# Threshold attention before a squared-ReLU feed-forward: where the weight sums are widened and multiplied in, and the order of a period's steps

## The chip, the cores and the metric

The kernel runs on one core of one Trainium2 chip, as one launch. The metric is the device time in microseconds; a kernel's time is the median of its runs.

## The reference, cut to what matters

```python
# attention: 8 batches, 8 heads, 576 positions, 64 values per head
scores = q @ k.T / 8                                   # per batch and head
thresh = max(scores, axis=-1) - tau                    # tau = 0.02
scores = where(scores >= thresh, scores, -1e9)
attn = exp(scores - max(scores))
attn = attn / (sum(attn, axis=-1) + 1e-9)
x = (attn @ v) laid out as (4608 tokens, 512)
# feed-forward
h = maximum(x @ w_in, 0)                               # w_in 512 x 2048
out = h * h @ w_out                                    # w_out 2048 x 512
```

The activations are float32. The two feed-forward matrices arrive as 64-bit floats, and the kernel turns them into float32 itself.

## The kernel before

The program has two stages: attention, whose result goes to DRAM as `xT`, and the feed-forward, which reads it back. Everything on the chip is ordered by hand: each engine carries out its instructions in the order in which the program issues them, and waits only for what it needs.

**The feed-forward** computes both layers as a two-level seven-product scheme (`inner`, line 689, called by `hidden_layer`, line 800, and `output_layer`, line 918), with 49 products where 64 would be plain. Its operands are sums of blocks of the matrices and of the inputs. The sums of `w_in` are made by GpSimd during attention: the generator `sums` (line 249) yields 44 additions of 128x512, and `prepare_x` (line 761) 12 more for the first 512 tokens. `sums_step` (line 570) makes one of them. The first layer's matmuls are line 812, the second's line 947.

**Attention** works on 144 units. A unit is 128 query rows of a pair of heads (32 pairs: 4 units each, and for every two pairs one more with the 64 rows that remain of both). `period(p)` (line 607), for p from -2 to 74, handles units A=2p and B=2p+1, and the weights and products of earlier units: m=p-2 is the pair of units whose product is made in this period. For each unit:

- *Scores* (`scores`, line 434): 64x512 matmuls of queries and keys into PSUM, steps `SA` and `SB`. The sign is turned by a scale, so that the largest score is the smallest value.
- *Minimum* (`top`, line 452): VectorE copies the scores of one head from PSUM to SBUF and takes each row's minimum on the way. There are two heads, so `topA0`, `topA1`, `topB0`, `topB1`.
- *Threshold* (`least`, line 459): GpSimd adds tau to the two minima, `leastA`, `leastB`.
- *Power* (line 462): ScalarE takes the exponential, `powA0` to `powB1`.
- *Mask* (line 467): VectorE zeroes what is beyond the threshold and sums the rest per row, `maskA0` to `maskB1`. It needs the power and the threshold.
- *Sum* (lines 474 and 477): `over` adds 1e-9 on GpSimd, `inv` inverts on VectorE, both one period after the masks, for both units at once.
- *Turning the weights* (`fill`, line 499; `half_turn`, line 375): the weights of the two units are 18 blocks of 128x128, turned on TensorE in three groups: `V` (8 blocks) and `W` (2 blocks) in the period after the masks, `U` (8) in the one after that. `V` and `U` share one PSUM tile; `W` uses the PSUM banks 2 and 3 of `sc`. ScalarE copies each group to the SBUF tile `wT` (`filled`, line 523): `eV`, `eW`, `eU`. `wT` has two buffers.
- *The inverse sums* are turned with `W`: eight 64x64 matmuls (line 515) of the inverse sum, spread by a zero step over 64 columns, with the identity. They land beside the two blocks of `W`, and `eW` copies them to blocks 10 and 11 of `wT` (`SCALE_AT`).
- *Product* (`values`, line 532): step `PV`, weights times values into banks 0 and 5 of `sc`.
- *x* (`given_out`, line 634): VectorE multiplies both heads' products by the turned inverse sums while it moves them from PSUM to SBUF (line 638). Then the loads of later values are issued (`valued`), and the outputs to `xT` (`give_x`, issued by `ask`, line 578).

The six banks of `sc` are shared. Scores of A lie in banks 0 and 5 with the rest of their columns in 1 and 4, those of B in 2 and 3 with rests in 1 and 4; the turned queries and keys of the next pair (`T`, line 397, evicted by `eT`, lines 402 and 410) in 1 and 4; `W` in 2 and 3; the product in 0 and 5. The helper `touch` (line 354) makes an instruction wait for those of other engines in the same bank. After `eT` the loads of the queries or keys of a later pair are issued.

The order of a period's steps is one of two lists of names: `CONVERTING` (line 596) for periods 2 to 34, in which 32 blocks of the feed-forward matrices are fetched (`fetch`) and converted in six steps (`c1` and `c2` on ScalarE, `c3` on GpSimd, `c4` and `c5` on VectorE, `c6` on GpSimd, with a write-back by line 247 for half of them), and `PLAIN` (line 592) for the others. In plain periods from 35 on, `s1` makes one of the 56 additions, and up to period 59 `s2` a second one. All DMAs but a few at the start are issued by SyncE (SP), in the order of the program.

Of the kernel before, what the change touches and what calls it, by code (L numbers as in the profile page):

```python
# [48 lines left out]
def kernel(  # L49
# [25 lines left out]
    nc = tc.nc  # L75
# [423 lines left out]
    def fill(m, f, pt, at=None):  # L499

        first, count = FILLS[f]
        if m not in wT:
            wT[m] = sb.tile([P, (2 * CH + 2) * P], FP32, tag="wT", bufs=W_RING, name="wT")
        for i, (u, c) in enumerate(FIRST[first : first + count]):
            half_turn(pt, i, weights[2 * m + u][:, c, :, :].rearrange("p j d -> p (j d)"), at)
        if f == "W":
            rs = smalls.pop(m)
            for j in range(2):
                for r in range(2):
                    rows = ds(r * HALF, HALF)  # L510
                    for u in range(2):
                        one = rs[rows, 3, 2 * u + j : 2 * u + j + 1]
                        wide = bass.AP(tensor=one.tensor, offset=one.offset, ap=[one.ap[0], [0, D]])
                        to = pt[ds(u * D, D), r, ts(count + j, HALF)]
                        made = nc.tensor.matmul(to, wide, ident[rows, rows], start=True, stop=True)  # L515
                        touch("turns", made, at and at + r * BANK, BANK)

    def filled(m, f, pt, at=None):

# [81 lines left out]
    def spots():  # L601
# [5 lines left out]
    def period(p):  # L607

        A, B_, a, b = 2 * p, 2 * p + 1, 2 * p - 2, 2 * p - 1
        m, turns = p - 2, TURNS.get(p, ())  # L610
        late, pt = {"W": []}, {}

        def fills(f, m):
            if has(2 * m):
                pt[f] = pt_pool.tile([P, 2, BANK], FP32, tag="pt", name="pt")
                fill(m, f, pt[f])

        def evict(f, m):
            if has(2 * m):
                filled(m, f, pt[f], 2 * BANK if f == "W" else None)  # L620

        def W():
            if has(2 * m + 2):
                pt["W"] = middle()
                fill(m + 1, "W", pt["W"], 2 * BANK)

        def turn_some():
            late["turn"] = [turn(g // 2, g % 2, spots()) for g in turns]

        def PV():  # L630
            if has(2 * m):
                values(m)

        def given_out():
            if has(2 * m):
                x = sb.tile([P, 2, P], FP32, tag="x", bufs=2, name="x")
                for j in range(2):
                    made = nc.vector.tensor_tensor(  # L638
                        out=x[:, j, :], in0=sc[:, ds(5 * j * BANK, P)], in1=wT[m][:, ts(SCALE_AT + j, P)], op=ALU.mult
                    )  # L640
                    touch("x", made, 5 * j * BANK, P, m)
                wT.pop(m)
                valued(m)
                give_x(m, x)
# [18 lines left out]
        steps = {  # L663
            "U": lambda: fills("U", m), "V": lambda: fills("V", m + 1), "W": W, "T": turn_some,
            "eU": lambda: evict("U", m), "eV": lambda: evict("V", m + 1), "eW": lambda: evict("W", m + 1),
            "eT": lambda: every("turn"),
            "SA": scored_a, "SB": scored_b,
            "PV": PV, "x": given_out,
            "c1": lambda: convert1(begun(p)), "c2": lambda: convert2(begun(p)),
            "c3": lambda: convert3(begun(p - 1)), "c4": lambda: convert4(begun(p - 1)),  # L670
            "c5": lambda: convert5(begun(p - 1)), "c6": lambda: convert6(begun(p - 1)),
            "s1": lambda: sums_due(p) and sums_step(), "s2": lambda: sums_due(p) and p < 60 and sums_step(), "fetch": lambda: fetch(begun(p + 2)),
        }
        steps["over"] = lambda: do(a, "over")
        steps["inv"] = lambda: do(a, "inverse")
        for letter, n in (("A", A), ("B", B_)):
            for what, name in (("least", "least"),):
                steps[what + letter] = lambda n=n, name=name: do(n, name)
            for what, name in (("top", "top"), ("pow", "power"), ("mask", "mask")):
                for j in range(2):  # L680
                    steps[f"{what}{letter}{j}"] = lambda n=n, name=name, j=j: do(n, name, j)
        for name in CONVERTING if converts(p) else PLAIN:
            steps[name]()
        for n in (A, B_):
            if has(n) and units[n][1] == FULL:
                for i in units[n][0]:
                    turned.pop(i)
# [522 lines left out]
```

## Time and profile before

| what | value |
|---|---|
| median of 3 runs | 1318.03 us (1316.82 to 1320.18) |
| span of the profiled execution | 1314.0 us |
| first matmul of layer 1 (line 812) | 519.45 us |
| busy over the span: PE, weight loads, VectorE, ScalarE, GpSimd | 97%, 87%, 77%, 65%, 64% |
| granted TensorE clock, mean | 0.998 |
| mask (line 467) | 288 times, 229.6 us |
| power (line 462) | 288 times, 208.2 us |
| minimum (line 452) | 288 times, 205.5 us |
| product (line 532) | 5760 matmuls, 176.7 us |
| evictions of weights (line 523), 128x1024 | 144 times, 146.6 us |
| x (line 638) | 144 times of 128x128, 285 ns each |
| inverse sums turned (line 515) | 1152 matmuls, 33.2 us |

PE, VectorE, ScalarE and GpSimd (POOL in the profile) work side by side, so their busy times overlap and don't add up to the span. Consecutive instructions of one engine overlap at their ends as well, so a run of them is better read by the distance of their starts than by their durations. In rows of the timeline the first number is the start in microseconds, the second the time from there to the end of the group, then follow engine, line, operation, tiles and shapes; in brackets stands how long the engine was idle before and what it waited for.

### The profile page before, as it was taken

To read this page: it belongs to the slowest core of one execution; us is meant where nothing else is said; L and a number is where in the kernel's file an instruction comes from. 1 tells how busy PE (TensorE), PEld (TensorE's weight loads), DVE (VectorE), ACT (ScalarE), POOL (GpSimd) and SP (SyncE) were. 2 spreads that over 40 slices of the span, in tenths; PEclk is the share of its full clock that TensorE was granted. 3 is DMA by queue.
4 is the path that set the end of the run, shared out by engine and by line. 5 is a ranking of instruction groups with operands and counts; after the bars stand their busy time and mean duration, and the time that the engine had idled before them with its cause. 6 is when DMAs were issued, how large, how long until landed. Compare 5 with 4: busy or idle time off the path is not lost.

```text
span 1314.0 us, 47792 instructions
## 1 busy us (share of the span) xinstructions
PE 1277.6 (97%) x19483; PEld 1141.4 (87%) x19483; DVE 1016.3 (77%) x2497; ACT 849.6 (65%) x1464; POOL 839.0 (64%) x958
## 2 busy tenths in 40 slices
PE   7999999899999999999999999999999999999998
PEld 5666666677777777999999999999999999999998
DVE  5999999999999996877887788777656654665463
ACT  5999999888989886566756675665524322432240
POOL 1444444455555421778987888758777777777775
PEclk9999999999999999999999999999999999999999
DMA  5555566544433322466656655669645135423411
GB/s 135 143 160 142 155 174 182 149 103 99 101 78 86 77 60 46 148 206 192 195 180 210 197 187 179 193 232 394 249 161 161 48 115 162 161 63 100 161 33 33
DMA packets 247035, 192.12 MB, mean 146 GB/s; under 512 B 97184, under 2 KB 195488, under 8 KB 246816
## 3 DMA queue, kind: packets, MB, share of 16 engines
q1 hardware_dynamic: 245360, 188.63, 47.4%
q8 instruction: 153, 2.51, 0.8%
q10 hardware_dynamic: 1456, 0.44, 0.1%
q14 instruction: 66, 0.54, 0.1%
HBM read 116.65 MB, written 72.35 MB: 144 GB/s over the span
## 4 chain that ended last, share of the span: by engine, by line
PE 85%; ACT 8%; DVE 3%; issue 2%; DMA 1%; SPq 1%; POOL 0%; ACTq 0%; DVEq 0%; POOLq 0%
PE ph L812 30%; PE po L947 28%; PE sc L434 9%; PE sc L532 8%; PE pt L379 5%; ACT arena L523 3%; ACT arena L462 3%; PE sc L397 2%; PE sc L515 2%; DVE arena L452 1%; PE sc L379 1%; DMA wall<-w 1%; ACT arena L402 1%; DVE arena L467 0%; DMA arena<-in_k_dram 0%
## 5 line engine op out<-in xcount | busy, mean ns | idle before, releaser
L125 POOL TENSOR_TENSOR arena<-arena 128x512 f32<-128x512 f32 (+1 forms) x314 | 378.0, 1222 | 134.5 <-DVE arena L125 120.5
L947 PE MATMUL po<-wall,arena 128*128 128x128 f32 x3528 | 395.0, 275 | 1.6 <-ACT arena L724 1.4
L947 PEld LDWEIGHTS po<-wall,arena 128*128 128x128 f32 x3528 | 394.3, 192 | 2.2 <-ACT arena L724 1.8
L812 PE MATMUL ph<-arena,wall 128*128 128x128 f32 x3528 | 394.2, 275 | 0.7 <-DVE arena L638 0.7
L812 PEld LDWEIGHTS ph<-arena,wall 128*128 128x128 f32 x3528 | 394.0, 192 | 0.8 <-issue 0.8
L125 DVE TENSOR_TENSOR arena<-ph,arena 128x512 f32<-128x512 f32 x378 | 256.4, 689 | 86.2 <-PE ph L812 66.0
L122 POOL TENSOR_TENSOR arena<-arena 128x128 f32<-128x128 f32 (+2 forms) x314 | 255.2, 814 | 48.6 <-DMA arena<-w 31.9
L125 DVE TENSOR_TENSOR arena<-po,arena 128x128 f32<-128x128 f32 x378 | 108.4, 290 | 167.6 <-PE po L947 163.4
L467 DVE SCALAR_TENSOR_TENSOR arena<-arena 128x576 f32<-128x576 f32 x288 | 229.6, 817 | 2.7 <-ACT arena L462 1.7
L462 ACT ACTIVATE arena<-arena 128x576 f32<-128x576 f32 x288 | 208.2, 778 | 14.1 <-DVE arena L452 7.0
L452 DVE TENSOR_SCALAR_CACHE_REDUCE arena<-sc 128x576 f32<-128x576 f32 x288 | 205.5, 751 | 13.3 <-ACT arena L523 5.5
L758 ACT COPY c<-arena 128x512 f32<-128x512 f32 (+1 forms) x303 | 173.5, 579 | 50.4 <-DVE arena L122 41.3
L532 PEld LDWEIGHTS sc<-arena 64*64 64x64 f32 x5760 | 154.0, 133 | 55.3 <-DVE arena L452 28.7
L532 PE MATMUL sc<-arena 64*64 64x128 f32 (+1 forms) x5760 | 176.7, 263 | 18.1 <-DVE arena L452 11.6
L122 DVE TENSOR_TENSOR arena<-arena,c 128x512 f32<-128x512 f32 (+1 forms) x267 | 174.9, 663 | 6.1 <-ACT c L758 4.0
L434 PE MATMUL sc<-arena 64*64 64x64 f32 (+1 forms) x2304 | 167.4, 414 | 5.6 <-ACT arena L402 5.6
L523 ACT COPY arena<-pt 128x1024 f32<-128x1024 f32 x144 | 146.6, 1018 | 24.8 <-PE pt L379 24.4
L724 ACT COPY arena<-po 128x128 f32<-128x128 f32 x63 | 16.6, 264 | 186.4 <-PE po L947 183.7
L459 POOL TENSOR_SCALAR arena<-arena,tau_p 128x2 f32<-128x2 f32 x144 | 75.1, 521 | 73.4 <-DVE arena L452 67.8
L724 ACT COPY arena<-ph 128x512 f32<-128x512 f32 x63 | 36.6, 581 | 124.2 <-PE ph L812 123.5
L379 PEld LDWEIGHTS pt<-ident,arena 64*128 64x128 f32 x2304 | 83.1, 139 | 38.2 <-ACT arena L523 25.6
L434 PEld LDWEIGHTS sc<-arena 64*64 64x64 f32 x2304 | 59.2, 134 | 52.2 <-ACT arena L402 26.4
(46 smaller groups left out, 896.1 us busy)
## 6 DMA issues: line engine op xcount, KB each, us to landing
g<-arena SPq DMA_DIRECT2D x144, 256.0 KB, 2.4
arena<-g SPq DMA_DIRECT2D x144, 256.0 KB, 4.4
w<-arena SPq DMA_DIRECT2D x60, 256.0 KB, 2.4
wall<-w SPq DMA_DIRECT2D x49, 256.0 KB, 5.2
arena<-w SPq DMA_DIRECT2D x44, 256.0 KB, 3.2
arena<-in_v_dram SPq DMA_DIRECT2D x32, 288.0 KB, 3.6
out_dram<-arena SPq DMA_DIRECT2D x70, 128.0 KB, 2.2
arena<-in_q_dram SPq DMA_DIRECT2D x64, 128.0 KB, 3.2
```

The costliest lines, as they stand in the source:

```text
L122: e.tensor_tensor(out=out, in0=x, in1=y, op=ALU.subtract)
L125: e.tensor_tensor(out=out, in0=x, in1=y, op=ALU.add)
L379: made = nc.tensor.transpose(pt[:, r, ts(slot, HALF)], of[rows, :], ident[rows, rows])
L434: made = nc.tensor.matmul(sc[at, ds(to, count)], lhs, kT[rows, ds(at_k, count)], start=True, stop=True)
L452: made = nc.vector.tensor_scalar(out=s[:, j, :], in0=sc[:, ds(at, S)], scalar1=1.0, scalar2=None, op0=ALU.mult, op1=ALU.min, accum_out=nmx ...
L462: nc.scalar.activation(out=w[:, :, j, :], in_=of(j), func=AF.Exp, bias=nmx[:, j : j + 1], scale=-1.0)
L467: nc.vector.scalar_tensor_tensor(out=w[:, :, j, :], in0=of(j), scalar=thr[:, j : j + 1], in1=w[:, :, j, :], op0=ALU.is_le, op1=ALU.mult, a ...
L523: touch("weights", nc.scalar.copy(joined(to), whole(pt, 0, count)), at, 2 * BANK, m)
L532: made = nc.tensor.matmul(sc[ds(u * D, D), ds(5 * j * BANK + row, count)], loaded_v[i][rows, (c - (u != j)) % CH, :], wT[m][rows, ds(weigh ...
L758: nc.scalar.copy(c, y)
L812: nc.tensor.matmul(to[:, j, :], W_IN[m, k][:, ts(j, P)], of[k][:, m - 1, :], start=(not more and j == 0), stop=True, skip_group_check=True,)
L947: nc.tensor.matmul(to, g[:, j, :], w[:, j, :], start=(not more and j == 0), stop=(j == 3), skip_group_check=True)
```

## The change

The inverse sums are no longer turned by matmuls of their own. A new step `spread` has GpSimd copy them, each value repeated 64 times, into blocks 10 and 11 of `wT`; `W` then turns these two blocks in place like two more blocks of weights (8 matmuls of two instructions each go, 4 transposes come), and `eW` copies them back as before. In `x`, VectorE multiplies the product of head 0 as before; that of head 1 is copied from PSUM by ScalarE, and a new step `xs` multiplies it on GpSimd and hands the outputs over. Both orders of steps are new. The second addition `s2` is made in every even period instead of every period below 60, and stands directly behind the first. Two small edits let `c2` stand anywhere in the order.

```diff
     def convert1(m):
         ...
         parts[m] = (lo, hi, a)
-        raws.pop(m)
 
     def convert2(m):
-        if m in parts:
-            lo = parts[m][0]
+        if m in raws or m in parts:
+            lo = pick(raws[m], 0) if m in raws else parts[m][0]
             nc.scalar.activation(out=lo, in_=lo.bitcast(U32), func=AF.Copy, bias=0.0, scale=2.0**-29)
 
     def convert6(m):
         ...
         lo, hi, a = parts.pop(m)
+        raws.pop(m)
 
     def fill(m, f, pt, at=None):
         ...
         if f == "W":
-            rs = smalls.pop(m)
             for j in range(2):
-                for r in range(2):
-                    rows = ds(r * HALF, HALF)
-                    for u in range(2):
-                        one = rs[rows, 3, 2 * u + j : 2 * u + j + 1]
-                        wide = bass.AP(tensor=one.tensor, offset=one.offset, ap=[one.ap[0], [0, D]])
-                        to = pt[ds(u * D, D), r, ts(count + j, HALF)]
-                        made = nc.tensor.matmul(to, wide, ident[rows, rows], start=True, stop=True)
-                        touch("turns", made, at and at + r * BANK, BANK)
+                half_turn(pt, count + j, wT[m][:, ts(SCALE_AT + j, P)], at)
+
+    def widen(m):
+
+        if m not in wT:
+            wT[m] = sb.tile([P, (2 * CH + 2) * P], FP32, tag="wT", bufs=W_RING, name="wT")
+        one = smalls.pop(m)[:, 3, 0:1]
+        wide = bass.AP(tensor=one.tensor, offset=one.offset, ap=[one.ap[0], [1, 2], [2, 2], [0, D]])
+        to = wT[m][:, ds(SCALE_AT * P, 2 * P)].rearrange("p (j u d) -> p j u d", j=2, u=2)
+        nc.gpsimd.tensor_copy(out=to, in_=wide)
 
     PLAIN = """
-        SA c3 T topA0 over U eU s1 SB topA1 powA1 leastA topB0 powB0 c1 s2 PV c4 V fetch
-        inv powA0 c5 topB1 powB1 eT maskA1 x W eV maskA0 leastB c2 c6 eW maskB0 maskB1
+        fetch U SA topA1 over s1 s2 topA0 SB topB1 inv eU powA1 V topB0 leastA spread PV powA0 maskA1 leastB maskA0 eV T powB1 x maskB1 powB0 xs maskB0 eT W eW
     """.split()
     CONVERTING = """
-        fetch c3 SA c1 SB topA1 over s1 U topA0 c2 powA1 topB0 topB1 eU leastA maskA1
-        leastB inv powA0 PV powB0 W maskA0 x powB1 maskB0 T c4 c5 maskB1 eT V c6 eW eV
+        fetch c1 T SA topA1 c3 topA0 U eU powA1 SB topB0 over topB1 powA0 c4 powB0 PV eT inv leastA maskA1 x powB1 leastB spread V eV maskA0 W maskB0 c5 c6 eW maskB1 xs c2
     """.split()
 
         def given_out():
             if has(2 * m):
                 x = sb.tile([P, 2, P], FP32, tag="x", bufs=2, name="x")
+                by_vector = (0,)
                 for j in range(2):
-                    made = nc.vector.tensor_tensor(
-                        out=x[:, j, :], in0=sc[:, ds(5 * j * BANK, P)], in1=wT[m][:, ts(SCALE_AT + j, P)], op=ALU.mult
-                    )
+                    by = sc[:, ds(5 * j * BANK, P)], wT[m][:, ts(SCALE_AT + j, P)]
+                    if j in by_vector:
+                        made = nc.vector.tensor_tensor(out=x[:, j, :], in0=by[0], in1=by[1], op=ALU.mult)
+                    else:
+                        made = nc.scalar.copy(x[:, j, :], by[0])
                     touch("x", made, 5 * j * BANK, P, m)
+                late["x"] = x, [j for j in range(2) if j not in by_vector], wT[m]
                 wT.pop(m)
                 valued(m)
+
+        def scaled_x():
+            if has(2 * m):
+                x, js, by = late["x"]
...
+                for j in js if len(js) == 1 else ():
+                    nc.gpsimd.tensor_tensor(out=x[:, j, :], in0=x[:, j, :], in1=by[:, ts(SCALE_AT + j, P)], op=ALU.mult)
                 give_x(m, x)
             ask(False)
 
         steps = {
             ...
-            "PV": PV, "x": given_out,
+            "PV": PV, "x": given_out, "xs": scaled_x,
             ...
-            "s1": lambda: sums_due(p) and sums_step(), "s2": lambda: sums_due(p) and p < 60 and sums_step(), ...
+            "s1": lambda: sums_due(p) and sums_step(), "s2": lambda: sums_due(p) and p % 2 == 0 and sums_step(), ...
         }
+        steps["spread"] = lambda: has(2 * m + 2) and widen(m + 1)
```

By engine, a plain period now issues:

| engine | before | after |
|---|---|---|
| PE | SA T U SB PV V W | U SA SB V PV T W |
| VectorE | topA0 topA1 topB0 inv topB1 maskA1 x maskA0 maskB0 maskB1 | topA1 topA0 topB1 inv topB0 maskA1 maskA0 x maskB1 maskB0 |
| ScalarE | eU powA1 powB0 powA0 powB1 eT eV eW | eU powA1 powA0 eV powB1 x powB0 eT eW |
| GpSimd | over s1 leastA s2 leastB | over s1 s2 leastA spread leastB xs |

and a converting one:

| engine | before | after |
|---|---|---|
| PE | SA SB U PV W T V | T SA U SB PV V W |
| VectorE | topA1 topA0 topB0 topB1 maskA1 inv maskA0 x maskB0 c4 c5 maskB1 | topA1 topA0 topB0 topB1 c4 inv maskA1 x maskA0 maskB0 c5 maskB1 |
| ScalarE | c1 c2 powA1 eU powA0 powB0 powB1 eT eW eV | c1 eU powA1 powA0 powB0 eT x powB1 eV eW c2 |
| GpSimd | c3 over leastA leastB c6 | c3 over leastA leastB spread c6 xs |

More of the change, by code (lines that the diff above doesn't have):

```diff
@@ L636, in given_out @@
                 x = sb.tile([P, 2, P], FP32, tag="x", bufs=2, name="x")
+                by_vector = (0,)
                 for j in range(2):
-                    made = nc.vector.tensor_tensor(
-                        out=x[:, j, :], in0=sc[:, ds(5 * j * BANK, P)], in1=wT[m][:, ts(SCALE_AT + j, P)], op=ALU.mult
-                    )
+                    by = sc[:, ds(5 * j * BANK, P)], wT[m][:, ts(SCALE_AT + j, P)]
[3 more added lines that the diff above has]
+                        made = nc.scalar.copy(x[:, j, :], by[0])
                     touch("x", made, 5 * j * BANK, P, m)
+                late["x"] = x, [j for j in range(2) if j not in by_vector], wT[m]
                 wT.pop(m)
                 valued(m)
+        def scaled_x():
+            if has(2 * m):
+                x, js, by = late["x"]
+                if len(js) == 2:
+                    nc.gpsimd.tensor_tensor(
+                        out=x[:, :, :].rearrange("p j q -> p (j q)"), in0=x[:, :, :].rearrange("p j q -> p (j q)"),
+                        in1=by[:, ds(SCALE_AT * P, 2 * P)], op=ALU.mult,
+                    )
+                for j in js if len(js) == 1 else ():
+                    nc.gpsimd.tensor_tensor(out=x[:, j, :], in0=x[:, j, :], in1=by[:, ts(SCALE_AT + j, P)], op=ALU.mult)
                 give_x(m, x)
@@ L671, in period @@
             "c5": lambda: convert5(begun(p - 1)), "c6": lambda: convert6(begun(p - 1)),
-            "s1": lambda: sums_due(p) and sums_step(), "s2": lambda: sums_due(p) and p < 60 and sums_step(), "fetch": lambda: fetch(begun(p + 2)),
+            "s1": lambda: sums_due(p) and sums_step(), "s2": lambda: sums_due(p) and p % 2 == 0 and sums_step(), "fetch": lambda: fetch(begun(p + 2)),
         }
+        steps["spread"] = lambda: has(2 * m + 2) and widen(m + 1)
         steps["over"] = lambda: do(a, "over")
```

## The prediction

> **What bounds the kernel now.** I read the busy tenths first, then three windows, the times at which the sums' epsilon is added (one line 474 per period, so its starts are the period marks), and then one period instruction by instruction.
>
> ```profile
> PE   7999999899999999999999999999999999999998
> PEld 5666666677777777999999999999999999999998
> DVE  5999999999999996877887788777656654665463
> ...
> 100.00:150.00 50.00, 46.34 (x1164) 31.83 (x1158) 49.37 (x144) 47.43 (x77) 22.08 (x33) 1.00 0.53 141
> 400.00:450.00 50.00, 49.35 (x1322) 37.35 (x1320) 47.99 (x145) 44.62 (x70) 25.73 (x37) 1.00 0.37 86
> 600.00:700.00 100.00, 100.00 (x898) 100.00 (x898) 77.25 (x122) 69.36 (x125) 84.82 (x101) 1.00 0.62 198
> ```
>
> The columns of a window are PE, weight loads, VectorE, ScalarE, GpSimd. From about 520 us on, matmul and weight load are full and nothing in the change touches them, so only attention (first layer-1 matmul at 519.45 us) can move. In it the converting periods are full on VectorE (49.37 of 50) and nearly on ScalarE; the plain ones are full on PE (49.35), with VectorE close behind.
>
> ```profile
> 41.20 0.23 POOL L474 TENSOR_SCALAR arena<-arena 128x4 f32<-128x4 f32 x1
> ...
> 269.13 0.23 POOL L474 TENSOR_SCALAR arena<-arena 128x4 f32<-128x4 f32 x1
> ...
> 512.02 0.23 POOL L474 TENSOR_SCALAR arena<-arena 128x4 f32<-128x4 f32 x1 [2.83 <-DVE arena L467]
> ```
>
> From 41.20 to 269.13 lie 31 converting periods, 7.353 us each; from there to 512.02 lie 37 plain ones, 6.565 each. In steps between such marks most plain periods take 6.43 to 6.57, and one in nine some 7.14 (once 7.44), where line 434 waits for a late line 402.
>
> One plain period on PE, by starts:
>
> ```profile
> 407.37 1.09 PE L434 MATMUL sc<-arena 64*64 64x512 f32 x8
> 408.28 2.46 PE L532 MATMUL sc<-arena 64*64 64x128 f32 x72
> 410.67 0.71 PE L379 MATMUL pt<-ident,arena 64*128 64x64 f32 x16
> 411.22 0.29 PE L379 MATMUL sc<-ident,arena 64*128 64x64 f32 x4
> 411.44 0.46 PE L515 MATMUL sc<-ident,arena 64*64 64x64 f32 x16
> 411.72 1.27 PE L434 MATMUL sc<-arena 64*64 64x512 f32 x24
> 412.92 0.47 PE L397 MATMUL sc<-ident,arena 64*128 64x64 f32 x8
> 413.23 0.71 PE L379 MATMUL pt<-ident,arena 64*128 64x64 f32 x16
> 413.87 1.09 PE L434 MATMUL sc<-arena 64*64 64x512 f32 x8
> ```
>
> Groups follow without a gap: 6.50 us of work in 6.50. VectorE's starts in the same period give 6.14 of work and 0.31 of waits, ScalarE's 6.12. In the converting period from 156.46, VectorE's starts run through to 163.79, 7.33 us, with no wait: four minima (line 452) 2.71, four masks (line 467) 2.96, inverse 0.20, two products (line 638) 0.40, two conversion steps 0.45 and 0.61. ScalarE takes 7.41 from one line 205 (156.47) to the next (163.88), 0.30 of it the wait below, so 7.11 of work where keys are turned; the period before, with queries, gives 7.00.
>
> ```profile
> 161.71 0.70 ACT L410 COPY arena<-sc 128x256 f32<-128x256 f32 x2 [0.30 <-PE sc L397]
> ```
>
> **A cost the busy shares hide** stands at 271 us:
>
> ```profile
> 270.96 1.28 POOL L122 TENSOR_TENSOR wall<-wall 128x512 f32<-128x512 f32 x1
> ...
> 271.63 1.22 DVE L467 SCALAR_TENSOR_TENSOR arena<-arena 128x576 f32<-128x576 f32 x1
> ...
> 272.21 0.79 POOL L459 TENSOR_SCALAR arena<-arena,tau_p 128x2 f32<-128x2 f32 x1
> ```
>
> A mask takes 0.81 as a rule. This one started while GpSimd added weights and took 0.41 longer, free 0.20 before that addition ended. In turn the small line 459 took 0.79 instead of 0.29 because a mask ran. Five masks in the run are longer than 0.9 (271.63, 278.17, 284.77, 318.09, 377.26). So a mask and a GpSimd instruction exclude each other; a GpSimd instruction holds a mask for about its duration less 0.20. The Trainium skill's page "SBUF — State Buffer", section "Who interferes with whom", says that a VectorE instruction with two SBUF inputs and a GpSimd one reading SBUF block each other for the whole instruction, the second to issue waiting. By that rule the three holds in (5) would grow by 0.5 together and the sum would be some 1327 (19 even periods 0.5 longer, 18 odd ones 0.2); the trace agrees on the blocking, and its 0.41 decides on the length.
>
> **The change, part by part.**
> (1) PE loses 8 matmuls per period (16 instructions, 411.44 to 411.72: 0.28) and gains 4 transposes, 0.14 at the 0.55 for 16 of line 379, up to 0.22 as the 4 at 411.22 take. I take 0.10 gained: plain PE work 6.40.
> (2) VectorE loses one of two products, 0.20 per period: 7.33 to 7.13 converting, 6.14 to 5.94 plain.
> (3) ScalarE gains a 128x128 copy out of PSUM. The nearest row is line 724's 264 ns for this shape; since ScalarE's instructions overlap (two 128x256 of line 402 in 0.82, 0.47 each), it adds between 0.17 and 0.26. I take 0.17, as for a run of instructions: 7.28 converting with keys, 7.17 with queries, 6.29 plain.
> (4) GpSimd gains the widening copy, 128x256 from 4 values. No row has it: between 0.29 (128x128 select at the start) and 0.61 (128x512, line 219); by size 0.40. And a 128x128 product, 0.46 as line 122's of that shape. Its load is no bound (13 to 29 of 50); what counts is where it lands. In plain order its queue is epsilon, sum, (every second period) sum, threshold A, widen, threshold B, product. In odd periods the widening falls under the last minimum, which reads PSUM; threshold B (hold 0.1, as the converting period shows: inverse to mask 0.20 instead of 0.09) and product (0.46-0.20=0.26, of which 0.20 lies under VectorE's own product) hold masks for 0.16, and VectorE has 0.46 to spare against PE's 6.40.
> (5) The second sum now stands ahead of threshold A. From the period at 308.71: epsilon starts 0.17 later, the sum 0.31 after that, the next instruction 1.25 later, another sum some 1.27, threshold 0.30: ready at 3.30, while minima and inverse end at 2.80. So in 19 even periods (36 to 72) the first mask, and behind it on VectorE every other mask and the product, is up to 0.50 late; about 0.26 is covered by the spare time of the odd period, which lets GpSimd start early. Then widening holds 0.20, threshold B 0.1, the product 0.06: 5.94+0.24+0.36=6.54. Without the cover, 6.80.
> (6) Plain mean: (6.40+6.54)/2=6.47. Queries that arrive late still stop line 434 one period in nine: the turn's eviction now stands behind all powers, 0.5 instead of some 0.65, +0.055. So 6.525 against 6.565: 37x0.04=1.5 us gained.
> (7) Converting: the turn goes to the period's head, which removes ScalarE's 0.30 wait, and ScalarE becomes the bound. Of nine periods four turn keys, four queries, one nothing (VectorE's 7.13): (4x7.28+4x7.17+7.13)/9=7.21, and 0.03 for waits that stay. Here threshold B's hold of 0.11 stays and the widening finds VectorE's product, which reads PSUM, behind the first mask. 31x(7.353-7.24)=3.5 gained. Bounds: 7.15 (-6) to 7.45 (+3), if widening and the moved c6 hold masks whole.
> (8) Moved DMA issues. Of a pair's keys, seven issues of some 0.6 stand behind the turn's eviction; in converting periods they now come before the weight's write-back (line 247) and the outputs (line 578), in plain ones behind outputs that wait for GpSimd's product. SP has 3.4 to 7.4 us of issues in a period of 7.3 (from 206.55, with queries, and from 198.37, with keys). One such backlog cost ScalarE 2.9 us in all (line 205 waiting for the write-back, three times); the next turn is two periods off, so I count nothing, -3 to +4 without that cover.
> (9) Ends: in the drain, the last-but-one product now stands behind transposes that need the last mask; before, it ran beside the masks (511.56). +0.5. The sums end in period 72 instead of 65; layer 1 needs them at 519, so nothing.
>
> Sum: -1.5-3.5+0.5=-4.5. Span 1314.0 to 1309.5; the median of the runs lies 4.0 above the span, so 1313.5.
>
> **Rivals.** (A) The masks wait for GpSimd. Mechanism: widening, threshold B and product each reach GpSimd while masks stand back to back, and take the port in between at whole length. Even plain periods: 5.94+0.50+0.40+0.23+0.26=7.33, odd 5.94+0.23+0.26=6.43, mean 6.88+0.05. 37x(6.93-6.565)=+13.5, converting even, drain +0.5: 1332. For: the 1.22 us mask; the old orders leave GpSimd idle while masks follow each other. Against: its holds were shorter than its instructions. It decides where the stalls of a period average over 0.6 (6.565 less 5.94); a zero-step copy much slower than 0.61 leads here too. The skill's rule above is this mechanism.
> (B) Time freed on VectorE and PE is only turned into waits: ScalarE's orders leave it waiting at the minima as now (0.5 of line 523 per plain period), converting periods stay at 7.33 and even and odd at 6.5: 1317 to 1319. The change then doesn't do what it is shaped for. For: three engines within 0.4 us of each other. Against: each shows no wait in the stage that it bounds.
> (C) No hold counts and the late threshold is covered: plain 6.33 on PE, converting 7.15: -8.7-6.3+0.5, 1303.5 to 1308, say 1306.
>
> **Chances.** Forecast 0.46 (own range 1309 to 1318), A 0.27, B 0.15, C 0.12. A measurement here can tell 0.3%, 4.0 us: faster is under 1314.1, slower over 1322.0. Faster: 0.36 of the forecast's 0.46 and C, 0.48. Same: the rest of it and most of B, 0.23. Slower: A and a little of B, 0.29. The range of 8 in 10 goes from between C and the forecast's edge, 1304, to A's middle, 1331.
>
> **What would show it.** Right: marks 7.2 to 7.3 apart to period 34 with VectorE waiting and ScalarE full; plain marks alternating near 6.4 and 6.55; layer 1 starting near 515. Line 467 longer than 0.9 in many periods, or a first mask waiting for line 459 by 0.5 and more, is A. Unchanged marks with new waits on line 462 or 523 are B. The widening far over 0.6, or line 397 waiting for loads, would break (4) or (8).

## The result and the profile after

The changed kernel takes 1300.51 us (median of 4 runs, 1299.34 to 1301.93) against 1318.24 (4 runs, 1316.82 to 1320.18) for the kernel before beside it: ratio 0.9871, 95% interval 0.9856 to 0.9885. It is faster by 1.3%, nearly four times what was forecast. The profiled execution spans 1299.1 us, against 1314.0; that is 14.9 less, where the medians differ by 17.7, since the execution behind the profile before was a quick one (more on this below). Lines below the first edit moved by 1 to 15: the eviction of weights is line 524, the product 533, x on VectorE 640, x on ScalarE 642, the widening 517, GpSimd's product 657, layer 1 line 827.

The first three views answer to those of before: the busy tenths, three windows (PE, weight loads, VectorE, ScalarE, GpSimd), and the marks, line 474.

```profile
PE   7999999999999999999999999999999999999998
PEld 4666666666766668999999999999999999999998
DVE  4999999999999995877787778777646654665463
```

```profile
100.00:150.00 50.00, 47.20 (x1128) 32.83 (x1124) 49.45 (x143) 50.00 (x88) 30.52 (x51) 1.00 0.55 143
400.00:450.00 50.00, 48.35 (x1238) 34.17 (x1236) 47.38 (x142) 46.60 (x80) 32.37 (x50) 1.00 0.35 78
600.00:700.00 100.00, 100.00 (x898) 100.00 (x897) 77.44 (x122) 64.69 (x116) 82.88 (x104) 1.00 0.62 199
```

```profile
45.35 0.23 POOL L474 TENSOR_SCALAR arena<-arena 128x4 f32<-128x4 f32 x1
...
261.85 0.23 POOL L474 TENSOR_SCALAR arena<-arena 128x4 f32<-128x4 f32 x1
...
498.01 0.23 POOL L474 TENSOR_SCALAR arena<-arena 128x4 f32<-128x4 f32 x1 [1.46 <-DVE arena L467]
```

The feed-forward's window is what it was. In the converting periods ScalarE is now full as well (50.00 of 50, before 47.43), in the plain ones PE has 1.6 us of 50 to spare. The distances of the marks say where the time went:

| stretch | before | after | gained | forecast |
|---|---|---|---|---|
| to the 4th mark | 41.20 | 45.35 | -4.15 | 0 |
| 31 converting periods | 227.93 (7.353 each) | 216.50 (6.984) | 11.43 | 3.5 |
| 37 plain periods | 242.89 (6.565) | 236.16 (6.383) | 6.73 | 1.5 |
| last mark to layer 1 | 7.43 | 6.90 | 0.53 | -0.5 |
| layer 1 to the end | 794.55 | 794.19 | 0.36 | 0 |

**A plain period on PE**, by starts:

```profile
399.43 0.52 PE L397 MATMUL sc<-ident,arena 64*128 64x64 f32 x10
399.79 0.41 PE L379 MATMUL sc<-ident,arena 64*128 64x64 f32 x8
400.04 0.66 PE L379 MATMUL pt<-ident,arena 64*128 64x64 f32 x16
400.66 2.30 PE L434 MATMUL sc<-arena 64*64 64x512 f32 x32
402.88 0.71 PE L379 MATMUL pt<-ident,arena 64*128 64x64 f32 x16
403.62 2.20 PE L533 MATMUL sc<-arena 64*64 64x128 f32 x72
405.75 0.47 PE L397 MATMUL sc<-ident,arena 64*128 64x64 f32 x8
```

From one turn of queries or keys (line 397) to the next it is 6.32, against 6.51 between the same two points of a period before (406.41 to 412.92). `W` with the widened sums takes 0.25 (399.79 to 400.04); before, `W` and the matmuls of line 515 took 0.50 (411.22 to 411.72).

**The second sum of an even period**: VectorE's first mask, and what GpSimd does ahead of it.

```profile
373.29 0.92 DVE L467 SCALAR_TENSOR_TENSOR arena<-arena 128x576 f32<-128x576 f32 x1 [0.19 <-POOL arena L459]
```

```profile
370.36 2.63 POOL L122 TENSOR_TENSOR wall<-wall 128x512 f32<-128x512 f32 x2
372.97 0.29 POOL L459 TENSOR_SCALAR arena<-arena,tau_p 128x2 f32<-128x2 f32 x1
373.21 0.39 POOL L517 COPY arena<-arena 128x256 f32<-128x256 f32 x1
```

The threshold does come late, as argued, but here the mask waits 0.19 for it and not 0.50, and the widening behind it costs the mask 0.11 (0.92 instead of 0.81). This row is at the low end: seven even periods show such a wait, of 0.19 to 0.51 (0.51 at 424.75). The 0.11 is met in 15 of the 18. By marks, even and odd periods take 6.62 and 6.16 in the mean.

**A converting period on VectorE**, and GpSimd beside it:

```profile
157.66 0.42 DVE L226 TENSOR_SCALAR arena<-arena 128x512 int32<-128x512 int32 x1
158.00 0.17 DVE L477 RECIPROCAL arena<-arena 128x4 f32<-128x4 f32 x1
158.08 0.79 DVE L467 SCALAR_TENSOR_TENSOR arena<-arena 128x576 f32<-128x576 f32 x1
```

```profile
158.30 0.83 POOL L517 COPY arena<-arena 128x256 f32<-128x256 f32 x1
```

Step `c4` (line 226) takes 0.34 to the next start, the inverse 0.08, where before they took 0.45 and 0.20. The widening, which takes 0.40 when nothing is in its way, waits for the first mask and passes in the stretch from 158.80 to 159.00, in which VectorE's x reads PSUM; the next mask starts at 159.00 and takes 0.81, undisturbed. From 154.95 to 161.82 VectorE needs 6.87 for its period, without a wait.

**ScalarE no longer waits for the turn**, but PE waits for loads, twice:

```profile
149.52 2.37 ACT L462 ACTIVATE arena<-arena 128x576 f32<-128x576 f32 x3
...
156.50 2.39 ACT L462 ACTIVATE arena<-arena 128x576 f32<-128x576 f32 x3
158.51 0.97 ACT L410 COPY arena<-sc 128x256 f32<-128x256 f32 x2
...
163.54 2.43 ACT L462 ACTIVATE arena<-arena 128x576 f32<-128x576 f32 x3
```

```profile
168.18 0.34 PE L397 MATMUL sc<-ident,arena 64*128 64x64 f32 x2 [0.69 <-DMA arena<-in_q_dram]
```

Line 410 had waited 0.30 for PE. From the powers (line 462) of one period to those of the next ScalarE now takes 6.98 with queries (149.52 to 156.50) and 7.04 with keys. The price is that a late load of queries now stops PE at the head of a period, with the scores behind it: the two waits (168.18 and 209.88, 0.69 each) make periods of 8.21 and 7.39 out of 6.87.

### The profile page after: what moved, and what is told of

Its sections match the earlier page's. It is cut to its first block, busy times and chain, and to the rows that moved or that the text cites. A ratio compares the mean times of both kernels' runs of the same rounds, so it can differ in the third digit from the quotient of the medians.

```text
span 1299.1 us, 46337 instructions
## 1 busy us (share of the span) xinstructions
PE 1260.8 (97%) x18619; PEld 1124.5 (87%) x18619; DVE 996.1 (77%) x2425; ACT 854.3 (66%) x1536; POOL 909.0 (70%) x1102
## 4 chain that ended last, share of the span: by engine, by line
PE 60%; DMA 2%; ACT 1%; DVE 0%; issue 0%; POOL 0%; ACTq 0%; SPq 0%
PE ph L827 29%; PE po L962 29%; DMA wall<-w 1%; PE sc L533 1%; PE sc L434 1%; DMA g<-arena 0%; PE pt L379 0%; ACT arena L806 0%; ACT arena L807 0%; DVE arena L452 0%; POOL arena L122 0%; ACT arena L524 0%; ACT c L773 0%; DVE arena L467 0%; PE sc L379 0%
## 5 line engine op out<-in xcount | busy, mean ns | idle before, releaser
L462 ACT ACTIVATE arena<-arena 128x576 f32<-128x576 f32 x288 | 223.0, 850 | 23.3 <-DVE arena L452 23.1
L533 PEld LDWEIGHTS sc<-arena 64*64 64x64 f32 x5760 | 144.7, 133 | 47.5 <-DVE arena L452 44.6
L434 PE MATMUL sc<-arena 64*64 64x64 f32 (+1 forms) x2304 | 171.5, 422 | 5.2 <-ACT arena L402 3.4
L533 PE MATMUL sc<-arena 64*64 64x128 f32 (+1 forms) x5760 | 160.7, 262 | 12.8 <-DVE arena L452 9.4
L524 ACT COPY arena<-pt 128x1024 f32<-128x1024 f32 x144 | 156.4, 1086 | 5.2 <-PE pt L379 5.1
L739 ACT COPY arena<-po 128x128 f32<-128x128 f32 x63 | 16.6, 264 | 186.5 <-PE po L962 183.7
L434 PEld LDWEIGHTS sc<-arena 64*64 64x64 f32 x2304 | 60.9, 135 | 55.0 <-issue 28.4
L379 PE MATMUL pt<-ident,arena 64*128 64x64 f32 x2304 | 101.2, 228 | 3.8 <-ACT arena L524 3.3
```

The lines of the kernel that those rows point to most:

```text
L379: made = nc.tensor.transpose(pt[:, r, ts(slot, HALF)], of[rows, :], ident[rows, rows])
L434: made = nc.tensor.matmul(sc[at, ds(to, count)], lhs, kT[rows, ds(at_k, count)], start=True, stop=True)
L462: nc.scalar.activation(out=w[:, :, j, :], in_=of(j), func=AF.Exp, bias=nmx[:, j : j + 1], scale=-1.0)
L524: touch("weights", nc.scalar.copy(joined(to), whole(pt, 0, count)), at, 2 * BANK, m)
L533: made = nc.tensor.matmul(sc[ds(u * D, D), ds(5 * j * BANK + row, count)], loaded_v[i][rows, (c - (u != j)) % CH, :], wT[m][rows, ds(weigh ...
```

## The experiments

**The four corners.** The change has two parts, the widening and the split of x, and two new orders. Four kernels hold one or two of these back.

*Orders alone:* x by VectorE for both heads, the sums by matmuls as before, no `spread`.

```diff
-                by_vector = (0,)
+                by_vector = (0, 1)
...
-                half_turn(pt, count + j, wT[m][:, ts(SCALE_AT + j, P)], at)
+            rs = smalls.pop(m)
+            for j in range(2):
...
+                        made = nc.tensor.matmul(to, wide, ident[rows, rows], start=True, stop=True)
...
-        steps["spread"] = lambda: has(2 * m + 2) and widen(m + 1)
+        steps["spread"] = lambda: None
```

> The changed kernel with both heads' product by VectorE and the inverse sums turned by matmuls as before: the new step orders alone. Theory W (a period lasts as long as the work of its longest queue, and the orders take waits out of it): converting periods on VectorE at 6.87+0.20=7.07, mean some 7.1 (before 7.35, changed 6.98); plain periods some 6.45 (6.565, 6.38); start 4 us later than before as in the changed kernel. 1318.2-7.7-4+3.6 = 1310. Rival O (the orders do everything, the parts nothing): 1300 to 1304. Rival P (the parts do everything): 1315 or more.

*Parts alone:* the orders of before with `spread` behind `inv` and `xs` last, and `s2` below period 60 as before.

```diff
     PLAIN = """
         SA c3 T topA0 over U eU s1 SB topA1 powA1 leastA topB0 powB0 c1 s2 PV c4 V fetch
-        inv powA0 c5 ... eW maskB0 maskB1
+        inv spread powA0 c5 ... eW maskB0 maskB1 xs
```

> The old orders with the widening put behind the inverse and the GpSimd product at the period's end: the parts alone. Theory W: converting VectorE 7.33-0.20=7.13, mean 7.2; plain periods still at 6.5 (PE gives 0.1, no more): 1318.2-5-2.4 = 1311. Rival O: 1316 to 1320. Rival P: 1300 to 1305. If the widening or the product hold masks for their whole length, masks (line 467) over 0.9 us in most periods and 1320 or more.

*x by VectorE:* only `by_vector = (0, 1)`.

> The changed kernel with both heads' product by VectorE; widening and orders stay. Theory W: VectorE is a bound of the converting period, 6.87+0.20: +0.15 to 0.20 in 31 periods, +5 to +6; plain +0.06, +2: 1307. Rival S (ScalarE, busy 50.00 of 50, is the only bound of converting periods): taking 0.14 of copy from it gives -4: 1296, and converting periods near 6.75 to 6.85.

*Sums by matmul:* only the matmuls in place of the widening.

> The changed kernel with the inverse sums turned by matmuls as before, no widening; the split product and the orders stay. Theory W: PE has room in converting periods (46 to 47 of 50) and some in plain ones, and GpSimd's widening held masks by 0.1 in even plain periods only: 0 to +3, 1300 to 1303. Rival (PE is the bound of plain periods, as the prediction took it): +0.10 to 0.14 in 37 periods, 1304 to 1306.

Measured, with the period lengths from the marks:

| orders | sums | x | median us | ratio to before | converting | plain |
|---|---|---|---|---|---|---|
| old | matmul | VectorE | 1318.24 | 1 | 7.353 | 6.565 |
| old | widened | split | 1335.77 | 1.0136 (1.0121 to 1.0151) | 7.356 | 7.056 |
| new | matmul | VectorE | 1316.96 | 0.9994 (0.9977 to 1.0011) | 7.130 | 6.645 |
| new | matmul | split | 1312.69 | 0.9965 (0.9953 to 0.9977) | 7.033 | 6.663 |
| new | widened | VectorE | 1308.77 | 0.993 (0.9915 to 0.9945) | 7.080 | 6.491 |
| new | widened | split | 1300.51 | 0.9871 (0.9856 to 0.9885) | 6.984 | 6.383 |

The ratios come from medians, the period lengths from one profiled execution each. Neither orders nor parts pay by themselves: the orders change nothing that can be measured (their ten runs spread from 1312 to 1324, and the profile is of one of 1313.8), the parts cost some 17.5 us, together they gain 17.7. I had expected 1311 for the parts alone, and missed by 25; 1310 for the orders alone, against 1317; and at most 1306 with the sums by matmul, against 1312.7. With x by VectorE it was 1307 and came to 1308.8.

In converting periods the shares simply add, once the orders are new: orders 0.22, split 0.10, widening 0.05. Two more profiles with the same converting order have 6.979 and 6.988 for the 6.984. In plain periods they do not. With the matmuls left in, the split gains nothing there (6.645 and 6.663), since PE bounds the period: its groups fill the 6.64 of one, but for some 0.2 ahead of the product. PE in the kernel with new orders, split x and matmuls:

```profile
406.46 0.29 PE L379 MATMUL sc<-ident,arena 64*128 64x64 f32 x4
406.68 0.46 PE L515 MATMUL sc<-ident,arena 64*64 64x64 f32 x16
407.07 0.71 PE L379 MATMUL pt<-ident,arena 64*128 64x64 f32 x16
```

Here `W` and its sums take 0.61 between starts (406.46 to 407.07), where the changed kernel takes 0.25: 0.36 less on PE, of which the period gives 0.28. Only then does the split pay 0.11 in plain periods too. The new order puts the transposes of `U` behind the matmuls, where the old one had scores; in the kernel before, that group took 0.50.

Why the parts lose in the old orders stands in the list of waits of that kernel's weight loads, from 280 to 460 us (total, times, longest):

```profile
PEld sc L434 <- ACT arena L642: 12.3, 19, 0.7
```

The next scores write banks 0 and 5, and must wait for ScalarE to have copied its product out of bank 5; in the old order that copy stands behind `eT`. On PE it shows as a longer group, of weight loads and matmuls together:

```profile
403.13 2.15 PE L434 MATMUL sc<-arena 64*64 64x512 f32 x24
405.22 0.52 PE L397 MATMUL sc<-ident,arena 64*128 64x64 f32 x10
```

The 24 take 2.09 to the next start, where they took 1.20 in the kernel before (411.72 to 412.92). In the changed kernel `T`, `W` and `U` stand between product and scores: the copy starts at 399.59, the scores at 400.66. And `W`, which in the old converting order is turned in the middle of the masks, waits for the widening there (0.44 to 0.48 from line 517, at 155.89 and 170.49): 7.356, none of the converting gain is left.

**How near the widening is to the edge.** It is made twice, into the same place.

```diff
         nc.gpsimd.tensor_copy(out=to, in_=wide)
+        nc.gpsimd.tensor_copy(out=to, in_=wide)
```

> The changed kernel with the widening copy issued twice. It tells what GpSimd's copies cost where masks follow each other. Theory H (a copy holds a mask for its length less 0.2, as the sum at 271 us did): the second copy, 0.35 to 0.40, adds 0.2 to 0.3 to converting and even plain periods: +9 to +13, 1310 to 1313. Rival N (a copy that repeats four values hardly reads and holds nothing): 1300 to 1302.

1324.6 us, ratio 1.004 (1.0028 to 1.0052); converting 7.463, plain 6.585. Both theories had it lower. Masks are held more: 108 of 288 are longer than 0.86, with 16.6 us above 0.81 in all, against 20 and 2.5 in the changed kernel. Some 10 of these 14 us lie in plain periods, which take 7.5 us longer in all. But converting periods lose 14.9 of the 24 us, and in one of them only one mask grows, by 0.13, and the period by 0.48. There the rest is a wait on PE, whose cause stands on GpSimd (31 such waits, 30.5 us in all, not all of which reach the period):

```profile
160.81 0.34 PE L379 MATMUL sc<-ident,arena 64*128 64x64 f32 x4 [0.93 <-POOL arena L518]
```

```profile
158.99 0.83 POOL L517 COPY arena<-arena 128x256 f32<-128x256 f32 x1
159.88 0.88 POOL L518 COPY arena<-arena 128x256 f32<-128x256 f32 x1
```

The second copy has missed the stretch in which x reads PSUM, waits for a mask, and ends at 160.76; `W` stands on PE and waits for it, with the turn and both units' scores behind. In the changed kernel the one copy ends at 159.13 and `W` starts at 159.12: it comes through with nothing to spare. So in converting periods a late widening is paid for on PE, more than on the masks.

**The second sum left out.** Of its 18 sums 16 are then made behind the last period, where layer 1 waits 14.17 and 2.28 us for them, so only the plain periods are compared.

```diff
-... "s2": lambda: sums_due(p) and p % 2 == 0 and sums_step(), ...
+... "s2": lambda: None, ...
```

> The changed kernel without the second sum in plain periods; the 16 sums left over are made between the stages, so only the marks from period 35 to 72 are read (236.2 us in the changed kernel), not the time. Theory of the prediction (in even periods the second sum makes the first threshold late by 0.5, half of it covered by time that the odd period leaves): 232 to 234. Rival L (the whole 0.5 counts in all 19 even periods): 226 to 228. Rival N (PE sets the plain period, the late threshold is covered): 235 to 236.

It ran once, with 1316.68 us in all; from the 35th mark to the 72nd 234.05 us against 236.16, 6.326 per period. Four other kernels with the plain order of the changed one take 236.1 to 236.5 there, so the difference stands out. The late threshold costs 2.1 us in the whole run, at the edge of the 232 to 234 expected. The 6.3 of PE remain.

**The price of four transposes.** The widened sums are turned twice.

```diff
-            for j in range(2):
-                half_turn(pt, count + j, wT[m][:, ts(SCALE_AT + j, P)], at)
+            for j in range(4):
+                half_turn(pt, count + j % 2, wT[m][:, ts(SCALE_AT + j % 2, P)], at)
```

> The two blocks of widened sums are turned twice, into the same place: 4 transposes more per period, nothing else. It asks two things: whether PE bounds the plain periods of the changed kernel, and what four transposes cost there. In the changed kernel the W group with its 8 transposes takes 0.25 us between starts, against 0.22 for 4 before and 0.14 by size from the group of 16. If PE bounds: plain 6.383 rises by the price, 0.03 to 0.14, that is 1 to 5 us in all; the price then is read from the W group and the matmul group that went must have cost 0.25 or so. If PE does not bound: plain unchanged within 0.02. Converting periods unchanged (6.98) in both cases, since VectorE and ScalarE bound them. Time 1301.5 to 1306 or 1300 to 1301.

1306.13 us, ratio 0.9906 (0.9889 to 0.9924). Plain 6.458, that is 0.075 more: PE does bound most of these periods. The group of now 12:

```profile
404.32 0.54 PE L379 MATMUL sc<-ident,arena 64*128 64x64 f32 x12
404.69 0.66 PE L379 MATMUL pt<-ident,arena 64*128 64x64 f32 x16
```

0.37 for 12 and 0.25 for 8: four transposes are worth 0.12, and the 0.22 that four of them took ahead of the matmuls of line 515 held 0.10 that went with those matmuls. The converting periods also took longer, 7.078, which neither theory had: most of it is in one period of 10.63 and in waits of line 397 for queries and keys (0.23 to 0.67, five times), and one of 1.46 on ScalarE for a write-back. The median converting period takes 6.88, against 6.92 in the changed kernel, so this is not put down to the edit; why those transfers came late here stays open.

**Where the converting 0.22 of the orders lies.** Step `c4` directly ahead of `c5`, as before the change, all else new.

```diff
     CONVERTING = """
-        ... powA0 c4 powB0 PV ... maskB0 c5 c6 ...
+        ... powA0 powB0 PV ... maskB0 c4 c5 c6 ...
```

> The changed kernel with the conversion step c4 directly ahead of c5 on VectorE, as before the change; c5 reads what c4 writes. Theory V (VectorE's work sets the converting period, and c4 took 0.45 ahead of c5 where it takes 0.34 ahead of the inverse): +0.1 in 33 periods, mean 7.08 for 6.98, 1303.5. Rival S (ScalarE alone sets it): mean 6.98, 1300 to 1301.

1308.8 us, ratio 0.9922 (0.9907 to 0.9938); converting 7.254, that is 0.27 more where I expected 0.1; plain 6.382, unchanged. VectorE shows two costs, of which only the one between `c4` and `c5` was there before the change:

```profile
157.29 0.29 DVE L640 TENSOR_TENSOR arena<-sc,arena 128x128 f32<-128x128 f32 x1 [0.26 <-PE sc L533]
...
158.97 0.42 DVE L226 TENSOR_SCALAR arena<-arena 128x512 int32<-128x512 int32 x1
159.43 0.69 DVE L234 SCALAR_TENSOR_TENSOR arena<-arena 128x512 int32<-128x512 int32 x1
```

`c5` starts 0.46 behind `c4`, whose result it reads; apart, `c4` took 0.34. And the product: PE may start it when the second minimum has freed the banks, and needs 2.1 to 2.3; VectorE then has two minima, an inverse and a mask to do, 2.16, and comes too early. In the changed kernel `c4` stands in between, 2.50 in all, and nothing waits. So `c4` was moved out of one wait and covers another.

*c4 behind the first mask* asks whether any place between does as well.

```diff
-        ... powA0 c4 powB0 PV eT inv leastA maskA1 x ...
+        ... powA0 powB0 PV eT inv leastA maskA1 c4 x ...
```

> Conversion step c4 between the first mask and the product, in converting periods only. With c4 directly ahead of c5 a typical period took 7.23 and 7.35 instead of 6.87: 0.12 because c5 reads what c4 has just written, and 0.22 to 0.34 because VectorE then came to the product before PE had finished it (0.26 idle, released by PE's line 533). If this reading is right, c4 behind the first mask covers the product again and is not next to c5: 6.87 to 6.92 typical, mean 6.98 to 7.05, time 1300 to 1303. Rival: what c4 covers is threshold B and the widening on GpSimd, which now fall under the first mask; then masks or W wait for them and a typical period takes 7.0 to 7.3, time 1303 to 1310. Plain periods unchanged (6.38).

1303.27 us, ratio 0.989 (0.9868 to 0.9912); 6.97 typical (mean 7.068), plain 6.381. Both costs of the last experiment are gone, and 0.10 of another comes. GpSimd in that kernel:

```profile
159.82 1.12 POOL L459 TENSOR_SCALAR arena<-arena,tau_p 128x2 f32<-128x2 f32 x1 [0.22 <-DVE arena L477]
160.89 0.39 POOL L517 COPY arena<-arena 128x256 f32<-128x256 f32 x1
```

Threshold B, 0.29 by itself, is kept out by the mask and by `c4` behind it, until 160.94; the widening follows, and the mask from 160.99 takes 0.91. The Trainium skill's page "SBUF — State Buffer", section "Who interferes with whom", names `tensor_scalar`, the operation of `c4`, among those that can take the ports that VectorE and GpSimd share, when its operands meet certain conditions; the 1.12 agrees, being 0.33 more than the 0.79 behind a mask alone.

**The start.** The order of before for the first plain periods, below 2, and then also for periods 2 and 3.

```diff
-        for name in CONVERTING if converts(p) else PLAIN:
+        for name in (START if p < 2 else FIRST_CONVERTING if p < 4 else CONVERTING if converts(p) else PLAIN):
```

(`START` and `FIRST_CONVERTING` are the lists of before with `spread` and `xs`; the first of the two kernels has only `START`.)

> The changed kernel with the old plain order (widening and GpSimd product put in) in the four periods before period 2, the new orders from there. In the changed kernel the fourth mark of line 474 stands at 45.35 us, before at 41.20. Theory (the new order is worse only at the start, where the turn stands last in its period and the next period's scores wait for it): the mark returns to 41 to 43 and the time falls by 2.5 to 4, 1296.5 to 1298. Rival (the start is longer because the first converting periods and GpSimd's new work hold it up, or because of TensorE's clock, which is 0.7 there in both): the mark stays at 44 to 46, 1300 to 1301.

> The old orders (with spread behind inv and xs at the end) for periods below 4: the plain one below 2, the converting one in 2 and 3. With the old order below 2 alone, the fourth mark fell from 45.35 to 43.29. If the rest of the distance to the 41.20 of before also lies in the order of the first periods, the fourth mark comes at 41 to 42 and the time falls by 1 to 2 us more, to 1298 to 1299. Rival: the first periods wait for the loads and the clock, not for the order; then the mark stays at 43 to 44 and the time at 1299.5 to 1301. Converting and plain periods as in the changed kernel in both cases (6.98 and 6.38).

| kernel | median us | ratio to before | span | 1st mark | 4th mark | between | converting |
|---|---|---|---|---|---|---|---|
| before | 1318.24 | 1 | 1314.0 | 16.68 | 41.20 | 24.52 | 7.353 |
| changed | 1300.51 | 0.9871 (0.9856 to 0.9885) | 1299.1 | 18.55 | 45.35 | 26.80 | 6.984 |
| old order below 2 | 1299.67 | 0.985 (0.9835 to 0.9864) | 1297.1 | 18.93 | 43.29 | 24.36 | 6.979 |
| old orders below 4 | 1300.09 | 0.9864 (0.9845 to 0.9884) | 1297.2 | 16.78 | 41.22 | 24.44 | 7.035 |

The 4th mark of the last kernel is where it was before, as expected, but by luck. The 1st mark moves by over 2 us with no difference in the program ahead of it: the two kernels of this experiment are the same up to there, and so are the changed kernel and the one without the second sum up to period 35. Their 1st marks:

```profile
18.55 0.23 POOL L474 TENSOR_SCALAR arena<-arena 128x4 f32<-128x4 f32 x1 [2.16 <-DVE arena L467]
```

```profile
16.17 0.23 POOL L474 TENSOR_SCALAR arena<-arena 128x4 f32<-128x4 f32 x1 [2.16 <-DVE arena L467]
```

From the 1st mark to the 4th both take the same, 26.80 and 26.82. So the order costs 2.3 of the 4.15 us, and the old order below period 2 brings all of that back. The other 1.9 lie ahead of the 1st mark, where two executions of the same steps differ by as much; no run here shows why. In the time little of it is seen. In the second kernel 1.6 us are lost again in converting periods, which wait for queries four times (0.19 to 1.56). The three intervals overlap, so none is called the better kernel.

## Why the prediction was wrong

The direction was right and the time was not: 1313.5 forecast, 1300.5 measured, below the range of 1309 to 1318 and below the wider one from 1304. The mechanisms mostly were as argued; the sizes in steps (7) and (1), and the holds on masks in (5), were not.

**Step (7) failed most**, by 8 us. It has ScalarE as the bound with 7.28 (keys) and 7.17 (queries), from (3), over VectorE's 7.13, from (2), and a mean of 7.24. That ScalarE becomes as full as VectorE is right, and its copy adds 0.14 where I took 0.17. But ScalarE's work with keys is 7.04, with queries 6.98, and VectorE's 6.87. I took work from the distances of starts less the waits in brackets. A bracketed wait counts from the end of the row before, and in a dense run the next row starts 0.10 earlier than that: the 0.30 at 161.71 was 0.40, as three powers take 2.41 to the next start there (from 159.30) and 2.01 in the kernel with only the orders changed (156.71 to 158.72). Another 0.09 of waiting lay around steps of the conversion. In that kernel the same work with keys takes 6.90, not 7.11:

```profile
155.80 1.01 ACT L532 COPY arena<-pt 128x1024 f32<-128x1024 f32 x1 [0.18 <-PE pt L379]
...
162.70 1.02 ACT L532 COPY arena<-pt 128x1024 f32<-128x1024 f32 x1
```

On VectorE, 0.45 for `c4` and 0.20 for the inverse, which I kept as work, held 0.11 of waiting for a result and 0.12 of threshold B's hold, which step (7) took to stay; both stem from what stands next to them, and the new order places them apart. 7.33 less 0.20, 0.11 and 0.12 is 6.90; 6.87 was measured.

**Step (1) is the other**, and gives the plain periods: 0.10 gained on PE, in truth 0.25 against the old place of the matmuls, 0.36 against the place that they would have had. I took four transposes at 0.14 to 0.22 beside a removal of 0.28; the 0.22 of the old group of four was itself inflated by its neighbour, as the group of 12 shows. 0.15 by 37 is 5.6 us, and step (6) was off by 5.2. In the prediction's own sum, though, less work on PE shortens only the odd periods, since the even ones stood at 6.54 by the late threshold and 0.36 of holds. They came down too since little of these holds was met: the masks of an even period lost some 0.11.

**(2) to (5) are right but for the holds.** x on VectorE 0.20 less; the widening 0.40 free of others, as estimated; GpSimd's product 0.45 against 0.46. In (5) the late threshold exists and is mostly covered: I had 0.14 left per even period over PE's own work, some 2.5 us in all; leaving the sum out gains 2.1. That the two are so near is in part luck, since (5)'s holds and PE's work were both taken too large. The holds of (4) and (5) are mostly absent, since it is mostly GpSimd that waits: its widening took 0.83 in a converting period, its threshold B 0.80 at 399.01, and the masks lost 2.5 us in the whole run. **Rival A** was therefore wrong here, but it is close by: it is what the second widening brings, only that in converting periods PE's `W` pays first. By the Trainium skill's rule of whole holds, from the page and section that the prediction names, it had 1327 (the 0.2 of odd periods counts only as cover lost to the even ones, as they stay under PE's 6.40; without it, 1323). No run of the changed kernel comes near either, because the instruction that blocks there mostly is the mask and the one that waits is GpSimd's; where GpSimd was first, the mask at 373.29 lost 0.11 of the 0.31 that the widening still had, and not the whole.

**Rival C**, 1306, had the plain 6.33 nearly right (6.383), and still 7.15 for converting periods. **(8)** is nearly right in sum and wrong in place: the three waits of ScalarE for write-backs, 2.9 us, are gone, and two of PE for queries have come, some 1.9. **(9)** has the wrong sign, -0.53 instead of +0.5, too small to be followed up. **Left out altogether** was the start: I read the stretch from the 4th mark on and let the periods ahead of it stand, though both orders change there as well. Of the 4.15 us lost there 2.3 are the order's.

Put together, the span was missed by 10.4: 7.9 in (7), 5.2 in (6), 1.0 in (9), 0.4 in the feed-forward, less 4.15 at the start. The other 2.6 of the 13.0 come from the step to the median: I added 4.0 to the span, and 1.4 was right. The 4.0 compared a quick execution with the median of others: in 37 executions of the kernel before that were timed beside the runs, the span lies 1.8 below the time, it is 1316.6 in the median, and only one has less than 1314.0.

## What to carry to other kernels

Take work from a stretch in which the engine is the bound, or from a kernel in which its waits are gone, and not from distances in a stretch where it waits for others: on VectorE two waits of about 0.1 in a converting period were worth as much as the product that left it. Before a price is taken from a row, look at its neighbours on the same engine; a result read by the next instruction, or a change of shape behind it, is in the distance too. Before the edges of a run are compared, see how far they move by themselves. And test an order and the parts that it was made for in all four corners: here each alone gains nothing or loses, since a new producer (widening, copy out of PSUM) pays only where its reader comes late enough.

## What the runs showed of the hardware

Two dependent steps of 128x512 on VectorE in a row cost 0.46 to the second's start, 0.34 with other work between. On PE 8 and 12 transposes of 64 rows take 0.25 and 0.37, but 4 ahead of 64x64 matmuls 0.22. In the rows shown, GpSimd's instructions get past masks that stand back to back only in the gaps: 0.40 of copying becomes 0.83 to 0.88, 0.29 of threshold 0.79 to 1.12, and a stretch of 0.20 in which VectorE reads PSUM was enough to let one in. A mask that starts while such an instruction is at work loses less than what is left of it: 0.10, with 0.29 left, in the kernel with `c4` behind the mask. The first 20 us of an execution can be 2.4 us longer or shorter with the same program (1st mark at 16.17 and 18.55).
